# Threshold attention, then a mixture of attention experts: second-stage scores over all 128 rows, from copies made by DMA

## The chip, the core and the metric

The kernel runs on one core of a Trainium2 chip. What counts is device time in microseconds (us) from start to end of one execution. The kernel before took a median of 1035.93 us in three runs (1033.07 to 1035.97).

## What is computed

Stage 1 is attention over batch 8, 8 heads, 576 positions (S), head width 64 (D), where only scores within `tau` of the row's maximum count. Stage 2 reads stage 1's output as `x` (8, 576, 512) and runs four attention experts (E), causal, over it. A gate picks two experts for each position.

```python
scores = scale * q @ k.T;  keep where scores >= max - tau;  x = softmax(kept) @ v
logits = x @ w_gate;  w = softmax over the two largest
for e in range(4):
    q, k, v = x @ wq[e], x @ wk[e], x @ wv[e]
    a = softmax(causal(scale * q @ k.T))
    out += w[e] * (a @ v @ wo[e])
```

## The kernel before

Scores need more precision than one pass of the fast matmul type (fp32r) gives. So each operand is split in a high part (the value rounded to fp32r) and a low part (the rest), and a product is the sum of three: high x high, high x low, low x high (`HHL`, line 321). The contraction runs over the head width, 64, which is half of TensorE's 128 rows.

Stage 1 works on 32 pairs of heads (four for each batch `b`), each in five steps `s`: four query tiles of 128 rows (t = 0 to 3) and one tail tile of the 64 last positions of both heads (t = 4). Its main tiles already use all 128 rows: `prep` (line 245) copies by DMA the high part of the queries over itself (`qt`: both halves of the rows hold the two parts) and the keys twice (`kt`), so that two matmuls, [q_high; q_low] x [k_high; k_high] and [q_high; q_low] x [k_low; k_low], give the sum (line 342). These DMAs are issued by SyncE (SP), as are all loads and stores; SP works its DMAs off in order.

Stage 2 of batch `b` begins once the batch's last pair is done (`begin`, line 668) and its work is spread over the stage-1 steps of batch `b + 1`. `project` (line 445) makes queries and keys of one pair of experts (`ep` is 0 or 1): both experts of the pair lie one over the other, expert j in rows 64 j to 64 j + 63, and the high and low part side by side in the tiles `Q2[b, ep, i]` (i = 0 queries, 1 keys), four buffers in all. ScalarE (ACT) makes the high part, VectorE (DVE) the low part (line 474). `values` (line 481) makes the values and the gate. `scores2` (line 540) makes the scores of one query tile t for both experts: for t < 4 each expert has a PSUM bank, and three matmuls of (t + 1) x 128 columns over its 64 rows; the two experts are issued in turn, and then one mask matmul (bf16, 128 columns) in each bank. The tail tile takes six matmuls of 288 columns over all rows (line 564) and is not changed. Then follow exp, scaling by the gate (`scale2`, GpSimd), transposes (`transp2`), the product with the values (`attnv2`) and the output projection (`output`).

The order is written by a planner. `matmul` and `queued` (lines 152 to 159) add up a clock `pe[1]` of what each TensorE instruction is reckoned to cost (columns / 2.4 + 11 ns, half of that for 64 rows, 190 ns for a change of shape). Each stage-1 step gets a share of `STEP` = 5700 ns; `fill` (line 730) puts stage-2 pieces in until the step's goal is reached. `tiled` (line 734), called once in each of the steps s = 1 to 4, places one score tile; a tail tile is placed at the end of a step. Lists hold what is due: `S2` score tiles (order `T_MID` = 4, 3, 2, 1, 0, for the last batch `T_END`), `T2` transposes (due 7000 ns after the scores), `A2` and `O2`. After the last stage-1 step the loop at line 805 works off the last batch. The framework then orders the instructions of each engine's queue by priority and by what it reckons to be ready, so matmuls of one tile can be moved apart.

Loads: `load_pair` (line 178) loads a pair's keys and queries (`km`, `qm`, one buffer) and values (`vm` and `vtz`, three buffers, `VB` = 3).

Of the kernel before, what the change touches and what calls it, by code (L numbers as in the profile page):

```python
# [9 lines left out]
F32 = mybir.dt.float32  # L10
F32R = mybir.dt.float32r
# [15 lines left out]
MORE = (2, 3)  # L27

AFTER_S2, AFTER_V, AFTER_T2, AFTER_AV2 = 7000, 8500, 1800, 2000
BETWEEN_S2, AFTER_V_END = 2000, 5000  # L30

AV_AT = {4: (0, 3), 6: (3, 5)}
XBUFS = (2, 2, 1, 1)
# [3 lines left out]
E_W2 = "P"  # L37
W_AT = (5, 6, 7, 8)
CUT = 2
T_END = (2, 3, 4, 1, 0)  # L40
T_MID = (4, 3, 2, 1, 0)
E_XH = "A"
E_PT2 = "A"
# [3 lines left out]
PFB = 2  # L47
PR = {
    "max": -0.509, "thr": -0.091, "exp": 0.327, "stt": -2.461, "sum": -1.419, "nrm": 0.098,
# [6 lines left out]
PPB = 4  # L56
P2B = 3
PTB = 9
PTTB = 4
VB = 3  # L60
E_PTT = "A"


# [1 line left out]
def kernel(  # L65
# [13 lines left out]
    nc = tc.nc  # L79
# [3 lines left out]
    P = 128  # L83
# [94 lines left out]
    def load_pair(n):  # L178
        b, hp = divmod(n, NPAIR)
        hs = slice(2 * hp, 2 * hp + 2)  # L180
        vm = one.tile([P, 2, R, D], F32, tag="vm", name=f"vm_{n}", bufs=VB)
        pr("ld")
        def load(dst, src):
            r = nc.sync.dma_start(dst, src)
            if n in (1, 2):
                tc.add_manual_dep(r.ins, SPREAD[0].name, NOSYNC, reason="order")
        for t, x in ((km, k), (qm, q)):
            load(t[:, :, :R], x[b, hs, :SM, :].rearrange("h (p r) d -> p h r d", r=R))
            load(t[:ST, :, R], x[b, hs, SM:, :].rearrange("h s d -> s h d"))
        load(vm, v[b, hs, :SM, :].rearrange("h (p r) d -> p h r d", r=R))  # L190
        for j, rows in enumerate((slice(0, ST), slice(ST, P))):
            load(vtz[n % VB][rows, j], v[b, 2 * hp + j, SM:, :])
        VS[n] = (vm, vtz[n % VB])

# [245 lines left out]


    q2ds = [zeros(f"q2d{i}") for i in range(2)]
    Q2, V2, GW, GT = {}, {}, {}, {}

    def project(b, ep, cs):

        first, last = cs[0] == 0, cs[-1] == NC - 1
        for i, (wh, wl) in enumerate(((wqh, wql), (wkh, wkl))):
            if last:
                Q2[b, ep, i] = one.tile([P, 2, S], F32R, tag=f"q2{ep}{i}", name=f"q2_{b}_{ep}_{i}")  # L450
            t = Q2.get((b, ep, i))
            es = slice(ep * P, (ep + 1) * P)
            for hf in range(2):
                cols = slice(hf * HS, (hf + 1) * HS)
                g = gbank(f"pj_{b}_{ep}_{i}_{hf}_{cs[0]}")
                pr("pj")
                mm = [(w, c, x) for c in cs for w, x in ((wh, 0), (wh, 1), (wl, 0))]
                for n, (w, c, x) in enumerate(mm):
                    matmul(g[:, :HS], w[:, c, es], XT[b, c][x][:, cols],
                                     start=(n == 0), stop=(n == len(mm) - 1))  # L460
                pr("q2")
                if not last:
                    if b not in Q2:
                        Q2[b] = two.tile([P, EP, 4, HS], F32, tag="kt", name=f"part_{b}")
                    copy(E_Q2, Q2[b][:, ep, 2 * i + hf], g[:, :HS])
                    yield 3 * len(cs) * HS
                    continue
                src = g[:, :HS]
                if not first:
                    src = Q2[b][:, ep, 2 * i + hf]  # L470
                    nc.vector.tensor_tensor(src, g[:, :HS], src, op=ALU.add)
                hi, lo = t[:, 0, cols], t[:, 1, cols]
                copy(E_Q2, hi, src)
                nc.vector.tensor_tensor(lo, src, hi.bitcast(F32), op=ALU.subtract)
                if i == 0 and hf == 1:
                    for j in range(2):
                        sl = slice(j * D, (j + 1) * D)
                        copy(E_QD, q2ds[ep][sl, :, j * ST:(j + 1) * ST], t[sl, :, SM:].bitcast(F32))
                yield 3 * len(cs) * HS
# [58 lines left out]
    Z = {}  # L538

    def scores2(b, t, ep):  # L540
        q2, k2 = Q2[b, ep, 0], Q2[b, ep, 1]
        nmx = small.tile([P, 2], F32, tag="nmx", name=f"nm2_{b}_{ep}_{t}")
        sm = small.tile([P, 2], F32, tag="sm", name=f"sm_{b}_{ep}_{t}")
        pr("s2")
        if t < R:
            w = (t + 1) * P
            if b == B - 1:
                g = ps_s.tile([P, 2, 512], F32, tag="s", name=f"s2_{b}_{t}_{ep}")
                gg = [g[:, j] for j in range(2)]
            else:  # L550
                gg = [gbank(f"s2_{b}_{t}_{ep}_{j}") for j in range(2)]
            for i, (x, y) in enumerate(HHL):
                for j in range(2):
                    sl = slice(j * D, (j + 1) * D)
                    matmul(gg[j][:, :w], q2[sl, x, t * P:w], k2[sl, y, :w], start=(i == 0), stop=False)
            for j in range(2):
                matmul(gg[j][:, t * P:w], ident_b, mask, start=False, stop=True)
            views = [g[:, :w] for g in gg]
        else:
            w = S  # L560
            g = ps_s.tile([P, 2, 512], F32, tag="s", name=f"s2_{b}_{t}_{ep}")
            for hf in range(2):
                cols = slice(hf * HS, (hf + 1) * HS)
                for i, (x, y) in enumerate(HHL):
                    matmul(g[:, hf, :HS], q2ds[ep][:, x], k2[:, y, cols],
                                     start=(i == 0), stop=(hf == 0 and i == 2))
            matmul(g[:, 1, HS - ST:HS], ident_b, mask2, start=False, stop=True)
            views = [g[:, :, :HS]]
        p2 = two.tile([P, 2 * SM], F32, tag="p2" if b < B - 1 else "pp", name=f"p2_{b}_{t}_{ep}",
                      bufs=P2B if b < B - 1 else PPB)  # L570
        for j, sv in enumerate(views):
            pr("nm2")
            nc.vector.tensor_reduce(nmx[:, j:j + 1], sv, axis=AX.X if t < R else AX.XY, op=ALU.max, negate=True)  # L573
            pr("p2")
            nc.scalar.activation(p2[:, j * SM:j * SM + w] if t < R else halves(p2[:, :S]), sv, AF.Exp, bias=nmx[:, j:j + 1],  # L575
                                 accum_out=sm[:, j:j + 1])
        P2[b, t, ep] = (p2, sm, w, len(views))
# [97 lines left out]
    def project_some():  # L675

        while proj:
            b, what, g = proj[0]
            if what == "v" and left.get(b - 1, 0) or any(x[1] == b - 1 and what == f"q{x[3]}" for x in S2):
                return False  # L680
            try:
                next(g)
                return True
            except StopIteration:
                proj.pop(0)
                if what[0] == "q":
                    S2.extend((0, b, t, int(what[1])) for t in (T_MID if b < B - 1 else T_END))
                elif what == "v":
                    T2[len(T2) - len(unscaled):] = [(pe[1] + (AFTER_V if now[0] < N else AFTER_V_END), *x) for x in unscaled]
                    while unscaled:  # L690
                        scale2(*unscaled.pop(0))
        return False

    def score_tile():
        _, b, t, ep = S2.pop(0)
        scores2(b, t, ep)
        if b in GW and not unscaled:
            scale2(b, t, ep)
        else:
            unscaled.append((b, t, ep))  # L700
        T2.append((pe[1] + AFTER_S2, b, t, ep))
# [32 lines left out]
    def tiled():  # L734

        for _ in range(2):
            if due(A2):
                value_tile()
        if S2 and S2[0][2] < R and len(T2) < P2B:
            score_tile()  # L740

    now[0] = -10
# [8 lines left out]
    for _ in prep(0):  # L751
        pass
    load_pair(1)
    pre = iter(())
    goal = 0.0
    for i in range(N + 2):
# [24 lines left out]
        if slot:  # L781
            m, at = (n, 4) if s == 4 else (n - 1, 6)
            if 0 <= m < NPR:
                attnv(m, TS[slice(*AV_AT[at])])
                if at == 6 and m % NPAIR == NPAIR - 1:
                    begin(m // NPAIR)
            tiled()
        else:
            next(tr, None)
            if s in MORE:  # L790
                tiled()
# [7 lines left out]
            proj.extend((B - 1, "p", project(B - 1, ep, range(CUT))) for ep in range(EP))  # L799
            proj.append((B - 1, "v", values(B - 1, range(CUT))))  # L800
        fill(goal)
        if S2 and S2[0][2] == R and len(T2) < P2B:
            score_tile()
        goal = min(goal, pe[1])

# [1 line left out]
    while proj or S2 or T2 or A2 or O2:  # L807
# [6 lines left out]
            value_tile()  # L814
        elif transposable():
            transpose_tile()
        elif S2 and len(T2) < (P2B if S2[0][1] < B - 1 else PPB) and pe[1] >= since:
            score_tile()
            since = pe[1] + BETWEEN_S2
        elif not project_some():  # L820
# [31 lines left out]
```

## Time and profile before

| | |
|---|---|
| median of 3 runs | 1035.93 us |
| the profiled execution | 1033.38 us |
| its span, first to last instruction | 1031.7 us |
| TensorE (PE) busy | 966.5 us, 94% |
| PE weight loads (PEld) | 863.5 us, 84% |
| VectorE (DVE) | 816.5 us, 79% |
| ScalarE (ACT) | 651.6 us, 63% |
| GpSimd (POOL) | 408.4 us, 40% |
| granted TensorE clock, mean | 0.99 |

Busy time of PE counts each matmul from its start to its modelled end; matmuls overlap, so the pitch from start to start says what one costs, not its duration. In the names of the trace `s<-q,q` are stage-2 score matmuls (t < 4), `s<-q,q2d` those of the tail tile, `s<-mask,ident_b` the mask, `s<-kt,qt` and `s<-hl,qd` the stage-1 scores, `t` and `tm` transposes, `pj` the projections, `av` products with values, `o` the output projection. A form such as 64*128 64x384 is the weights (rows * columns) and the moving operand.

### The profile page before, as it was taken

The page shows a single profiled execution, that of the slowest core. Times are in us where ns is not written, and L with a number is a line of the kernel's source. Part 1 is how long each engine was busy: PE and PEld are TensorE (multiplying, and loading weights), DVE is VectorE, ACT ScalarE, POOL GpSimd, SP SyncE. Part 2 cuts the span into 40 slices and gives each one's busy share as a digit, 9 for nine tenths or more (in the row PEclk, how much of TensorE's full clock was granted, in tenths as well). Part 3 has the DMA queues.
Part 4 walks back from the last instruction along what each step waited for, and adds up shares of the span by engine and source line. Part 5 has one row for each costly group of instructions (what it writes and reads, how often), then busy time and mean ns, then how long its engine had stood idle before and what let it go on. Part 6 is the DMA issues. An engine that isn't in the chain of part 4 may idle for free.

```text
span 1031.7 us, 26572 instructions
## 1 busy us (share of the span) xinstructions
PE 966.5 (94%) x9520; PEld 863.5 (84%) x9520; DVE 816.5 (79%) x2374; ACT 651.6 (63%) x1564; POOL 408.4 (40%) x700
## 2 busy tenths in 40 slices
PE   4778999999999999999999999999999999999998
PEld 3676898789888898888987898978988889888975
DVE  4778688877888779888789878887788877988564
ACT  3667566765667656765667656676566765676554
POOL 2556424533244334443344332453324533433122
PEclk9998999999999999999999999999999999999999
DMA  6555423344223443225343242334322344311101
GB/s 156 142 128 141 121 73 91 102 117 119 59 72 95 133 112 93 61 68 143 90 103 94 72 124 75 91 102 126 110 56 73 96 132 112 79 30 44 42 2 46
DMA packets 83891, 96.11 MB, mean 93 GB/s; under 512 B 29745, under 2 KB 54321, under 8 KB 83761
## 3 DMA queue, kind: packets, MB, share of 16 engines
q1 hardware_dynamic: 83296, 93.83, 34.5%
q8 instruction: 76, 1.25, 0.5%
q10 hardware_dynamic: 464, 0.59, 0.2%
q14 instruction: 55, 0.44, 0.1%
HBM read 30.42 MB, written 9.44 MB: 39 GB/s over the span
## 4 chain that ended last, share of the span: by engine, by line
PE 59%; DVE 17%; ACT 13%; issue 5%; POOL 4%; DMA 1%; SPq 0%; DVEq 0%; ACTq 0%; POOLq 0%
PE av L159 18%; PE s L159 13%; PE tm L162 8%; PE pj L159 7%; DVE pp L356 5%; PE v L159 4%; PE o L159 4%; ACT p L575 3%; ACT pp L354 3%; PE t L162 3%; DVE nmx L349 3%; DVE x L439 2%; ACT pt L144 2%; PE qkT L162 2%; POOL pp L364 2%
## 5 line engine op out<-in xcount | busy, mean ns | idle before, releaser
L364 POOL TENSOR_SCALAR pp<-pp,ss 128x576 f32<-128x576 f32 x288 | 212.8, 750 | 408.4 <-DVE ss L370 313.0
L356 DVE SCALAR_TENSOR_TENSOR pp<-s,thr,pp 128x576 f32<-128x576 f32 x288 | 233.0, 814 | 77.3 <-ACT pp L354 72.5
L354 ACT ACTIVATE pp<-s,nmx 128x576 f32<-128x576 f32 x288 | 213.7, 746 | 80.6 <-DVE nmx L349 76.8
L349 DVE TENSOR_REDUCE nmx<-s 128x1 f32<-128x576 f32 x288 | 215.8, 751 | 41.6 <-PE s L159 40.4
L159 PE MATMUL s<-kt,qt 128*128 128x288 f32 x1024 | 205.3, 319 | 5.8 <-DMA qt<-hl 5.4
L162 PE MATMUL tm<-ident,pp 128*128 128x128 f32 x1152 | 166.2, 278 | 22.1 <-POOL pp L364 15.8
L159 PE MATMUL av<-pt,vm 128*64 128x128 f32 (+1 forms) x2560 | 167.8, 267 | 0.0
L159 PEld LDWEIGHTS s<-kt,qt 128*128 128x128 f32 x1024 | 151.9, 194 | 15.5 <-DMA qt<-hl 5.7
L162 PEld LDWEIGHTS tm<-ident,pp 128*128 128x128 f32 x1152 | 136.1, 143 | 33.2 <-POOL pp L364 22.6
L159 PEld LDWEIGHTS av<-pt,vm 128*64 128x64 f32 x2560 | 140.0, 138 | 15.4 <-issue 11.4
L144 ACT COPY pt<-tm 128x512 f32<-128x512 f32 x199 | 113.6, 589 | 58.6 <-PE tm L162 56.3
L575 ACT ACTIVATE p<-s,nm 128x384 f32<-128x384 f32 (+3 forms) x144 | 78.9, 551 | 63.4 <-DVE nm L573 59.0
L589 POOL TENSOR_SCALAR p<-p,sm,gw 128x512 f32<-128x512 f32 (+3 forms) x128 | 77.1, 610 | 81.4 <-ACT pt L144 35.4
L140 ACT ACTIVATE x<-av 128x256 fp32r<-128x256 f32 (+1 forms) x96 | 48.0, 500 | 71.5 <-PE av L159 49.6
L573 DVE TENSOR_REDUCE nm<-s 128x1 f32<-128x384 f32 (+3 forms) x144 | 71.1, 513 | 24.2 <-PE s L159 21.4
L162 PE MATMUL t<-ident,p 128*128 128x128 f32 x384 | 61.1, 284 | 15.9 <-DVE ss L369 8.9
L159 PE MATMUL av<-ptt,vtz 128*64 128x128 f32 (+1 forms) x640 | 68.8, 263 | 0.0
L140 ACT ACTIVATE pt<-t 128x512 f32<-128x512 f32 (+2 forms) x112 | 57.9, 541 | 15.6 <-PE t L162 14.2
L159 PE MATMUL v<-wvh,x 128*128 128x260 f32 x320 | 64.8, 287 | 0.0
L162 PEld LDWEIGHTS t<-ident,p 128*128 128x128 f32 x384 | 43.0, 144 | 25.9 <-POOL p L589 14.3
L439 DVE TENSOR_TENSOR x<-av,x 128x256 fp32r<-128x256 f32 (+1 forms) x96 | 47.6, 495 | 19.2 <-ACT x L140 16.0
L159 PE MATMUL av<-pt,v 128*64 128x128 f32 (+1 forms) x896 | 57.9, 262 | 1.9 <-ACT p L575 1.2
(132 smaller groups left out, 1808.9 us busy)
## 6 DMA issues: line engine op xcount, KB each, us to landing
kt<-hl SPq DMA_DIRECT2D x252, 144.0 KB, 2.7
qt<-hl SPq DMA_DIRECT2D x128, 128.0 KB, 2.4
km<-in_k_dram SPq DMA_DIRECT2D x32, 256.0 KB, 3.0
qm<-in_q_dram SPq DMA_DIRECT2D x32, 256.0 KB, 3.2
vm<-in_v_dram SPq DMA_DIRECT2D x32, 256.0 KB, 2.8
out_dram<-ob SPq DMA_DIRECT2D x32, 256.0 KB, 2.4
km<-in_k_dram SPq DMA_DIRECT2D x32, 32.0 KB, 2.7
qm<-in_q_dram SPq DMA_DIRECT2D x32, 32.0 KB, 2.7
```

The source lines that it names most:

```text
L140: nc.scalar.activation(dst, src, AF.Copy)
L144: nc.any.tensor_copy(dst, src)
L159: queued(nc.tensor.matmul(out, x, y, **kw), x, ns if x.shape[0] == P else ns / 2)
L162: queued(nc.tensor.transpose(out, x, ident), x, 109)
L349: nc.vector.tensor_reduce(nmx[:, js], sv, axis=AX.XY, op=ALU.max, negate=True)
L354: nc.scalar.activation(e, sv, AF.Exp, bias=nmx[:, js])
L356: nc.vector.scalar_tensor_tensor(e, sv, thr[:, js], e, op0=ALU.is_ge, op1=ALU.mult, accum_out=ss[:, js])
L364: nc.gpsimd.tensor_scalar(p, p, ss[:, h:h + 1], 0.0, op0=ALU.mult, op1=ALU.add)
L439: nc.vector.tensor_tensor(xl, gs, xh.bitcast(F32), op=ALU.subtract)
L573: nc.vector.tensor_reduce(nmx[:, j:j + 1], sv, axis=AX.X if t < R else AX.XY, op=ALU.max, negate=True)
L575: nc.scalar.activation(p2[:, j * SM:j * SM + w] if t < R else halves(p2[:, :S]), sv, AF.Exp, bias=nmx[:, j:j + 1], accum_out=sm[:, j:j + 1])
L589: nc.gpsimd.tensor_scalar(p, p, sm[:, j:j + 1], gg[:, j:j + 1], op0=ALU.mult, op1=ALU.mult)
```

## The change

- `scores2` for t < 4 takes two matmuls over 128 rows for each expert in place of three over 64. The experts come one after the other, each with its mask behind its two matmuls.
- `spread2` makes the operands: twelve DMAs on SP for each pair of experts, 64 rows of 512 columns each (128 KB): the queries' high over low part (`q2x`), the keys' high over high and low over low (`k2x`). There is one buffer of each (`X2`). For the last pair of the last batch the free stage-1 buffers `qt` and `kt` are taken.
- `spread_next` issues these DMAs when the head of `S2` comes to another pair of experts. A score tile with t < 4 may be placed only `AFTER_SPREAD` = 6000 ns of the planner's clock later (`scorable`); tail tiles may at once.
- `Q2` has two buffers in place of four, so the queries and keys of pair 1 are projected into those of pair 0; `project_some` holds a projection until all score tiles left in `S2` are no tails and have their copies.
- `VB` is 2. Values are loaded by `load_values` in step s = 1, behind the `attnv` that last reads the buffer.
- `T_END` is (4, 2, 3, 1, 0) in place of (2, 3, 4, 1, 0).

```diff
-BETWEEN_S2, AFTER_V_END = 2000, 5000
+BETWEEN_S2, AFTER_V_END, AFTER_SPREAD = 2000, 5000, 6000
-T_END = (2, 3, 4, 1, 0)
+T_END = (4, 2, 3, 1, 0)
-VB = 3
+VB = 2
...
+    X2 = (const.tile([P, 2, SM], F32R, name="q2x"), const.tile([P, 2, 2, SM], F32R, name="k2x"))
+    def spread2(b, ep):
+        qs, ks = Q2[b, ep, 0], Q2[b, ep, 1]
+        heads = [slice(j * D, (j + 1) * D) for j in range(2)]
+        q2x, k2x = X2 if (b, ep) != (B - 1, EP - 1) else (
+            two.tile([P, 2, SM], F32R, tag="qt", name="q2x_end"),
+            two.tile([P, 2, 2, S], F32R, tag="kt", name="k2x_end")[:, :, :, :SM])
+        Q2[b, ep] = (q2x, k2x)
+        pr("dm2")
+        for j, sl in enumerate(heads):
+            for x, rows in enumerate(heads):
+                for dst, src in ((q2x[rows, j], qs[sl, x, :SM]), (k2x[heads[0], j, x], ks[sl, x, :SM]),
+                                 (k2x[heads[1], j, x], ks[sl, x, :SM])):
+                    nc.sync.dma_start(dst.bitcast(F32), src.bitcast(F32))
...
-                Q2[b, ep, i] = one.tile([P, 2, S], F32R, tag=f"q2{ep}{i}", name=f"q2_{b}_{ep}_{i}")
+                Q2[b, ep, i] = one.tile([P, 2, S], F32R, tag=f"q2{i}", name=f"q2_{b}_{ep}_{i}")
...
-            for i, (x, y) in enumerate(HHL):
-                for j in range(2):
-                    sl = slice(j * D, (j + 1) * D)
-                    matmul(gg[j][:, :w], q2[sl, x, t * P:w], k2[sl, y, :w], start=(i == 0), stop=False)
             for j in range(2):
+                for i in range(2):
+                    matmul(gg[j][:, :w], q2x[:, j, t * P:w], k2x[:, j, i, :w], start=(i == 0), stop=False)
                 matmul(gg[j][:, t * P:w], ident_b, mask, start=False, stop=True)
...
-            if what == "v" and left.get(b - 1, 0) or any(x[1] == b - 1 and what == f"q{x[3]}" for x in S2):
+            if what == "v" and left.get(b - 1, 0) or what[0] == "q" and any(x[2] == R or (x[1], x[3]) != spread[0] for x in S2):
...
+    spread = [None, 0.0]
+    def spread_next():
+        if S2:
+            key = (S2[0][1], S2[0][3])
+            if key != spread[0]:
+                spread2(*key)
+                spread[:] = key, pe[1] + AFTER_SPREAD
+    def scorable(tail):
+        return S2 and (S2[0][2] == R) == tail and (tail or pe[1] >= spread[1])
...
-        if S2 and S2[0][2] < R and len(T2) < P2B:
+        if scorable(False) and len(T2) < P2B:
...
+            if s == 1 and n + 1 < NPR:
+                load_values(n + 1)
```

## Rows read from the trace of the kernel before

**Rows 1.** Windows: stretch, length, busy us (instructions) by engine, granted clock, DMA, GB/s.
```profile
508.00:630.00 122.00, 118.10 (x1188) 106.35 (x1189) 100.49 (x293) 79.51 (x192) 48.66 (x80) 1.00 0.37 96
966.00:1000.00 34.00, 31.72 (x294) 28.48 (x293) 20.43 (x65) 14.61 (x42) 6.26 (x10) 0.96 0.05 17
1000.00:1031.70 31.70, 26.81 (x240) 19.48 (x238) 14.50 (x45) 16.37 (x51) 8.73 (x17) 0.98 0.11 38
```
**Rows 2.** Waits of PE, 508 to 630 us: waited in total, times, longest.
```profile
PE t L162 <- DVE ss L369: 1.3, 1, 1.3
```
**Rows 3.** Timeline of PE, undisturbed score tiles: start, length (us), instructions merged.
```profile
581.18 0.33 PE L159 MATMUL s<-q,q 64*128 64x128 f32 x2
...
581.18 0.55 PE L159 MATMUL s<-q,q 64*128 64x128 f32 x6
581.66 0.28 PE L159 MATMUL s<-mask,ident_b 128*128 128x128 bf16 x2
581.76 0.79 PE L159 MATMUL s<-kt,qt 128*128 128x288 f32 x4
...
994.91 0.63 PE L159 MATMUL s<-q,q 64*128 64x256 f32 x6
...
639.83 0.80 PE L159 MATMUL s<-q,q 64*128 64x384 f32 x6
...
630.37 0.96 PE L159 MATMUL s<-q,q 64*128 64x512 f32 x6
```
**Rows 4.** Timeline of PE, score tiles whose second bank came late.
```profile
540.78 0.80 PE L159 MATMUL s<-q,q 64*128 64x256 f32 x6
...
560.94 1.21 PE L159 MATMUL s<-q,q 64*128 64x384 f32 x6
...
569.47 0.62 PE L159 MATMUL s<-q,q 64*128 64x256 f32 x3
570.34 0.61 PE L159 MATMUL s<-q,q 64*128 64x256 f32 x3 [0.26 <-DVE zl L642]
```
**Rows 5.** Timeline of PE, matmuls over all 128 rows.
```profile
992.31 0.96 PE L159 MATMUL s<-q,q2d 128*128 128x288 f32 x6
993.11 0.20 PE L159 MATMUL s<-mask,ident_b 128*128 128x64 bf16 x1
993.15 0.51 PE L159 MATMUL pj<-x,wkh 128*128 128x288 f32 x2
...
572.54 0.40 PE L159 MATMUL o<-wol,zh 128*128 128x512 f32 x1
572.78 0.39 PE L159 MATMUL o<-woh,zl 128*128 128x512 f32 x1
...
625.40 1.04 PE L162 MATMUL tm<-ident,pp 128*128 128x128 f32 x8
```
**Rows 6.** The page, part 6: DMA issues, KB each, median us to landing.
```profile
qt<-hl SPq DMA_DIRECT2D x128, 128.0 KB, 2.4
```
**Rows 7.** Timeline of SP and DVE around the projection of expert pair 0.
```profile
617.79 0.46 DVE L474 TENSOR_TENSOR q<-pj,q 128x288 fp32r<-128x288 f32 x1 [0.59 <-ACT q L140]
...
619.68 2.48 SPq L282 DMA_DIRECT2D qt<-hl  x4
622.20 1.28 SPq L184 DMA_DIRECT2D km<-in_k_dram  x2
```
**Rows 8.** Timeline of PE and SP around expert pair 0's last tile and pair 1's first.
```profile
549.27 1.13 SPq L184 DMA_DIRECT2D vtz<-in_v_dram  x2
...
548.92 0.55 PE L159 MATMUL s<-q,q 64*128 64x128 f32 x6
...
555.21 0.96 PE L159 MATMUL s<-q,q 64*128 64x512 f32 x6
...
555.63 6.59 SPq L282 DMA_DIRECT2D kt<-hl  x8
...
574.61 0.38 PE L159 MATMUL s<-kt,qt 128*128 128x288 f32 x1
```

More of the change, by code (lines that the diff above doesn't have):

```diff
@@ L180, in load_pair @@
         hs = slice(2 * hp, 2 * hp + 2)
-        vm = one.tile([P, 2, R, D], F32, tag="vm", name=f"vm_{n}", bufs=VB)
         pr("ld")
@@ L189, in load_pair, with load_values, load @@
             load(t[:ST, :, R], x[b, hs, SM:, :].rearrange("h s d -> s h d"))
-        load(vm, v[b, hs, :SM, :].rearrange("h (p r) d -> p h r d", r=R))
+    def load_values(n):
+        b, hp = divmod(n, NPAIR)
+        vm = one.tile([P, 2, R, D], F32, tag="vm", name=f"vm_{n}", bufs=VB)
+        pr("ld")
+        def load(dst, src):
+            r = nc.sync.dma_start(dst, src)
+            if n < 2:
+                tc.add_manual_dep(r.ins, SPREAD[0].name, NOSYNC, reason="order")
+        load(vm, v[b, 2 * hp:2 * hp + 2, :SM, :].rearrange("h (p r) d -> p h r d", r=R))
         for j, rows in enumerate((slice(0, ST), slice(ST, P))):
@@ L540, in scores2 @@
     def scores2(b, t, ep):
-        q2, k2 = Q2[b, ep, 0], Q2[b, ep, 1]
         nmx = small.tile([P, 2], F32, tag="nmx", name=f"nm2_{b}_{ep}_{t}")
@@ L545, in scores2 @@
         if t < R:
+            q2x, k2x = Q2[b, ep]
             w = (t + 1) * P
@@ L564, in scores2 @@
                 for i, (x, y) in enumerate(HHL):
-                    matmul(g[:, hf, :HS], q2ds[ep][:, x], k2[:, y, cols],
+                    matmul(g[:, hf, :HS], q2ds[ep][:, x], Q2[b, ep, 1][:, y, cols],
                                      start=(i == 0), stop=(hf == 0 and i == 2))
@@ L687, in project_some @@
                     S2.extend((0, b, t, int(what[1])) for t in (T_MID if b < B - 1 else T_END))
+                    spread_next()
                 elif what == "v":
@@ L696, in score_tile @@
         scores2(b, t, ep)
+        spread_next()
         if b in GW and not unscaled:
@@ L753 @@
     load_pair(1)
+    load_values(0)
     pre = iter(())
@@ L784 @@
                 attnv(m, TS[slice(*AV_AT[at])])
+            if s == 1 and n + 1 < NPR:
+                load_values(n + 1)
+            if 0 <= m < NPR:
                 if at == 6 and m % NPAIR == NPAIR - 1:
@@ L801 @@
         fill(goal)
-        if S2 and S2[0][2] == R and len(T2) < P2B:
+        if scorable(True) and len(T2) < P2B:
             score_tile()
@@ L816 @@
             transpose_tile()
-        elif S2 and len(T2) < (P2B if S2[0][1] < B - 1 else PPB) and pe[1] >= since:
+        elif S2 and scorable(S2[0][2] == R) and len(T2) < (P2B if S2[0][1] < B - 1 else PPB) and pe[1] >= since:
             score_tile()
```

2 rows, old and new, of the table PR are left out of this document.

## The prediction

> **What bounds the kernel now.** I read the windows by stage first, then the waits of PE inside one batch, then the timeline of PE at each of the 64 score tiles that change, and last SP's timeline around the places where the new copies come. In the middle of the run PE is busy for 118.10 of 122 us at the full clock, DVE for 100.49, ACT for 79.51 [rows 1]; PE's longest wait there is 1.3 us, once [rows 2]. So PE's issue sets the time of a batch: a matmul fewer is gained, a stop of PE is lost. The end is different: from 966 us on PE is busy for 31.72 of 34 us and then 26.81 of 31.7 [rows 1], which leaves 7.2 us idle; there chains count as well.
>
> What a score tile costs is read from pitches. In an undisturbed tile the two experts' half-row matmuls start together: two have started by 581.20, and six of 128 columns end 0.55 us after the first start, with the masks 0.48 us after it and the next matmul 0.58 us after it [rows 3]. The masks start 0.07 us before the last score matmul ends, and the next matmul 0.10 us after them, so a tile costs its row's length plus 0.03 us: 0.58, 0.66, 0.83 and 0.99 us for 128, 256, 384 and 512 columns [rows 3], together 3.06 us. This overlap is lost where the second expert's PSUM bank comes late: 1.21 us against 0.80 at 384 columns, 0.80 against 0.63 at 256, and 1.48 us (569.47 to 570.95) against 0.63 at 256 [rows 3, 4]. In each of the seven batches 0 to 6, each of the three happens about once (8, 7 and 7 times); in the last batch the timeline shows no such tile.
>
> **The change, part by part.**
>
> *Matmuls.* Full-row pitches: 0.11 us for 128 columns ((1.04 - 0.27) / 7 in eight transposes, 0.27 the length of the last, an estimate), 0.133 for 288 (six in 0.80), 0.235 for 512 [rows 5]. Between them I put 0.12 for 256 and 0.177 for 384. A mask inside full-row work costs 0.04 us to the next start, and that matmul then takes 0.08 longer: two matmuls of 288 last 0.51 us where 0.133 + 0.295 are due [rows 5]. A tile after is four matmuls, a mask between at 0.12 and one behind at 0.04: 0.60, 0.64, 0.87 and 1.10 us, together 3.21. So six matmuls become four and an undisturbed set of four tiles still gets 0.15 us dearer; 16 sets make +2.4 us. (Full rows save some 0.15 us a tile of change between half and full rows, and lose the overlap.)
>
> What is gained is the lost overlap: 0.41 + 0.17 + 0.85 = 1.43 us a batch. Part of the third is a real wait, as its second bank is free only 0.87 us after the first start, when the two matmuls and the mask of the first expert are over at 0.36; then the tile still costs 0.87 + 0.24 + 0.04 = 1.15 us, 0.51 above an undisturbed one, and only 0.34 of the 0.85 comes back. Bounds: 0.92 to 1.43 a batch, 6.5 to 10.0 over seven. I take 8.4 (1.2 a batch), as the tiles of pair 1 fall into other steps (below). Net of the 2.4: **-6.0 us** (-4.1 to -7.6).
>
> The Trainium skill ("TensorEngine Tiling (Array Packing)", Theoretical Speedup) says that a contraction of at most 64 rows can gain up to 2x from row tiling, which speaks against this change; its Key Properties say that a change of the tiling mode drains the engine, which speaks for it. The trace shows both: starts together, and 0.48 us for three overlapped starts where 0.33 would do. The first rule alone is rival C.
>
> *Copies for pair 0.* Twelve DMAs of 128 KB like `qt`'s: four take SP 2.48 us, 0.62 each [rows 7], and one lands 2.4 us after its issue [rows 6]. They come behind the low part of the keys, ready at 618.25, and behind SP's running copies for stage 1, which end at 622.16 [rows 7]. The first six, which are all that expert 0 needs, land at 622.2 + 5 x 0.62 + 2.4 = 627.7; the last at 631.4. Tile t = 3 stands at 630.37 [rows 3], over 6000 ns later also by the planner, so it stays in its step. Expert 1's matmuls come 2 x 0.235 + 0.04 us later, at 630.9: 0.5 us too early. Bounds: none, if the framework puts other matmuls ahead; 3.1 us, if the next pair's four loads (two take 1.28 us [rows 7]) go ahead of the copies. Over seven batches 0 to 22 us; by the nearest row 3.5, and I take **+2**, since in these queues matmuls move apart where an operand is late.
>
> *Copies for pair 1.* There is one `X2`, so SP must wait until t = 0 of pair 0 has run (548.92 to 549.47), and the values' load moved to this step stands ahead until 550.4 [rows 8]. The first six land at 555.9, the last at 559.6. By the charges of lines 152 to 162 for what stands between them, the next step's call of `tiled` comes 4 to 5 us of the planner's clock after t = 0, less than 6000 ns, so t = 3 does not stand at 555.21 [rows 8] any more but one step on, where t = 2 stands now, 560.94 [rows 4], and each later tile of pair 1 moves one step. Its work ends before the next batch's begins, so this costs nothing; its cover is other stage-2 pieces. Bounds: 0, to 3.9 us a batch (expert 1 wanted at 555.7, landed at 559.6) if it stays in its step, 27 us in all. Value taken: **0**, with 0.8 us to spare.
>
> What is queued behind on SP: `kt`'s and `qt`'s copies for the next pair. At 555.63 they start up to 1.6 us late and would end at about 567 instead of 564.8; first used at 574.61 [rows 8]. Loads of keys and queries slip by up to 7.4 us, and values are loaded a pair ahead; no one waits at once. Q2's two buffers hold the projection of pair 1 until pair 0's copies are read: in the middle this comes some 20 us later, nothing.
>
> The Trainium skill ("DMA: Bandwidth & Descriptors", Issuing engines are not separate DMA queues) calls the sequencer's time to initiate a DMA usually small relative to the DMA. Here twelve issues take 7.4 us and one landing 2.4, so the trace disagrees. By the page the copies would land some 3 us after they start and the +2 would be 0.
>
> *The end.* After pair 0's queries and keys of the last batch, the tail, the values and half of pair 1's projection cover the 6000 ns; then copies land up to 11 x 0.62 + 2.4 = 9.2 us after the start, 3 us late for expert 1. Pair 1's projection must also wait for these copies before it is written back. But the values and the gate end earlier than now (only one score tile ahead instead of two), and 7.2 us of idle time are there to take it up. Bounds: -3 (half of that idle) to +6 (9.2 less the 3.2 us that four projection pieces of six 0.133 us cover). I take **+0.5**.
>
> *Start and two value buffers:* values of a pair are read a pair later; nothing, bounds -0.3 to +0.3, half a DMA issue.
>
> **Sum.** 1033.38 - 6.0 + 2.0 + 0 + 0.5 = 1029.9 us. The profiled execution is 2.5 us below the median shown; two of three runs lie there. I add 1.1 for that: **1031 us**.
>
> **Rivals.**
>
> A, *no change*: the late banks stay late under the new order, so that 0.92 a batch comes back (net -4.1) and pair 0's copies cost the 3.5 of the nearest row: 1033.38 - 4.1 + 3.5 + 0.5 = 1033.3. For it: PE still meets banks that others release. Against: the tiles move.
>
> B, *the score tiles wait on PE for the copies*. PE works in order, and behind a waiting score matmul stands the stage-1 work that sets the batch's time. With the loads ahead of pair 0's copies, 3.1 us a batch: 1033.38 - 6.0 + 21.7 + 0.5 = 1049.6; with pair 1 in its old step 1055. It decides from 1.2 us a batch on ((6.0 - 0.5 + 3.1) / 7). For it: only 0.5 us is missing for pair 0 as it is. Against: PE waits almost nowhere now.
>
> C, *half rows are simply cheaper*: if a set of four were worth three full-row matmuls for each width, not 3.06 us, four would cost a third more: 0.64 us a set (0.11 + 0.12 + 0.177 + 0.235), 10.3 over 16; with 8.4 back, 1033.38 + 10.3 - 8.4 + 2.5 = 1037.8. Against: the 0.48 us of rows 3.
>
> **Chances.** Forecast 0.50, A 0.23, B 0.22, C 0.05. About 0.3% (3.1 us) is what a measurement of this kernel can tell from no change. The forecast's own range is 1023 (-7.6, no wait, -3 at the end) to 1032; A is "same", B and C slower. With A and the lower half of B the range is 1023 to 1048. Faster 0.50, same 0.23, slower 0.27.
>
> **What would show it.** Matmuls named `s<-k2x,q2x`: 256 of 128*128; a 512-column tile about 1.1 us and a 128-column tile about 0.6 us to the next matmul. SP: twelve issues in 7.4 us. PE's waits: little put down to the copies. t = 3 of pair 1 about 11 us behind t = 0 of pair 0. The distance between the same stage-1 step of two batches some 0.6 us shorter ((6.0 - 2.0) / 7) shows the loop's part. The prediction is wrong if PE waits over 1.2 us a batch for the copies, or if the last 65 us get more than 6 us longer.

## The result, and the profile after

The changed kernel takes 1024.62 us (median of 4 runs, 1023.74 to 1025.70); the kernel before took 1035.68 beside it. The ratio is 0.9899, 95% interval 0.988 to 0.9918. Forecast were 1031 us, with a range of 1023 to 1048: the direction and the range held, but the gain is more than twice the forecast one (1.0% against 0.45%).

The profiled execution takes 1023.74 us, its span 1021.6. Where the 10 us between the spans lie is seen by cutting both at the start of the fifth and of the last pair of heads (the first matmul `s<-hl,qd` of each pair): the first four pairs take 110.6 us before and 107.2 after, the loop 828.0 and 812.5, the end 93.0 and 102.0.

Windows of the kernel after: the start, one batch, the end. Columns as in [rows 1].
```profile
0.00:107.00 107.00, 76.65 (x708) 66.77 (x708) 75.20 (x214) 64.36 (x128) 53.92 (x117) 0.95 0.58 149
...
497.70:620.10 122.40, 118.25 (x1177) 107.71 (x1176) 103.84 (x299) 77.69 (x187) 48.46 (x80) 0.99 0.48 121
919.70:1021.60 101.90, 91.24 (x801) 77.53 (x800) 60.75 (x184) 52.12 (x149) 26.19 (x43) 0.98 0.24 63
```
The same view of the kernel before, start and end (a batch stands in [rows 1]).
```profile
0.00:111.00 111.00, 81.00 (x711) 71.06 (x712) 75.28 (x214) 64.56 (x129) 54.22 (x118) 0.92 0.58 146
...
939.00:1031.70 92.70, 85.48 (x769) 72.55 (x767) 56.21 (x168) 48.70 (x134) 22.11 (x37) 0.98 0.08 27
```
The start is no part of the change: there are no score tiles of the second stage in it, and PE's time for as many instructions follows the granted clock (0.92 and 0.95 of 2.4 GHz). A second profile of the changed kernel took 111.6 us for it, with a span of 1023.9, so only the medians and the time from the fifth pair on are compared below. The end is 9 us longer: PE has 32 more instructions and 5.8 us more work in it, which the loop did before, and its idle time rose from 7.2 to 10.7 us. The batch shown is the longest; the seven between the pairs 1 and 29 take 102.2 us (the first), then 120.5, 119.2, 120.2, 122.4, 120.5 and 121.9. Before, all but the first take 122.4 to 122.9. Part of the length of the two longest, 122.4 and 121.9, is TensorE's clock. Right behind PE's waits for copies (1.00 and 1.42 us here, 2.0 us two batches later) the granted clock is at half, 1.2 GHz, for 3.4 us:
```profile
560.90:564.30 3.40, 3.38 (x16) 2.67 (x14) 2.40 (x7) 2.12 (x6) 0.75 (x1) 0.50 0.55 166
```
By an estimate (work that takes 3.4 us at half the clock takes 1.7 at the full one) the two stretches cost some 3 us. The second profile has none in the loop, and its two batches take 121.2 and 120.6 us.

The group of the new score matmuls after (busy time, mean ns; idle time just before them and what ended it):
```profile
L159 PE MATMUL s<-k2x,q2x 128*128 128x384 f32 (+3 forms) x240 | 64.9, 361 | 14.0 <-DMA q2x<-q 8.3 <-ACT p L598 2.4 <-ACT ptt L140 1.5
```
240 and not 256: the last pair of the last batch has tiles of its own name. Of PE's idle time of 14.0 us in front of them, 9.3 us are waits for the copies (8.3 on `q2x`, 1.0 on `k2x`).

An undisturbed 512-column tile after, in PE's timeline (start, length, instructions):
```profile
505.88 0.73 PE L159 MATMUL s<-k2x,q2x 128*128 128x512 f32 x2
506.45 0.23 PE L159 MATMUL s<-mask,ident_b 128*128 128x128 bf16 x1
506.49 0.71 PE L159 MATMUL s<-k2x,q2x 128*128 128x512 f32 x2
507.04 0.23 PE L159 MATMUL s<-mask,ident_b 128*128 128x128 bf16 x1
507.08 0.77 PE L159 MATMUL s<-kt,qt 128*128 128x288 f32 x4
```
It costs 1.20 us to the next matmul, where six half-row matmuls cost 0.99 [rows 3] and 1.10 were forecast. The others of this batch take 0.97, 0.75 and 0.64 us. By the starts of all matmuls from the fifth pair on (idle time counted apart), score tiles with all masks (those of the tail tiles too, 0.7 us) hold 59.6 us before and 63.3 us after. So the part of the change that was to give the gain gives none.

SP and PE around the second pair of experts in the batch shown, after:
```profile
545.74 4.38 SPq L290 DMA_DIRECT2D qt<-hl  x4
550.22 0.55 SPq L468 DMA_DIRECT2D q2x<-q  x1
550.81 1.23 SPq L468 DMA_DIRECT2D k2x<-q  x2
552.09 0.61 SPq L468 DMA_DIRECT2D q2x<-q  x1
552.74 2.61 SPq L468 DMA_DIRECT2D k2x<-q  x2
555.45 0.54 SPq L468 DMA_DIRECT2D q2x<-q  x1
556.03 1.34 SPq L468 DMA_DIRECT2D k2x<-q  x2
557.41 0.59 SPq L468 DMA_DIRECT2D q2x<-q  x1
558.05 1.24 SPq L468 DMA_DIRECT2D k2x<-q  x2
```
```profile
556.53 0.40 PE L159 MATMUL s<-k2x,q2x 128*128 128x512 f32 x1
557.93 0.47 PE L159 MATMUL s<-k2x,q2x 128*128 128x512 f32 x1 [1.00 <-DMA k2x<-q]
559.90 0.47 PE L159 MATMUL s<-k2x,q2x 128*128 128x512 f32 x1 [1.42 <-DMA q2x<-q]
```
The twelve issues take 9.1 us and the matmuls come into the middle of them. PE's waits over the whole run after:
```profile
PE s L159 <- DMA q2x<-q: 8.3, 6, 2.0
...
PE s L159 <- DVE pp L364: 4.9, 14, 0.6
```
With one wait of 1.0 us on `k2x`, PE waits 9.3 us for copies. All of it stands at tile t = 3 of the second pair of experts, in the batches 1 to 6. Yet the waits that came once a batch before are gone from batch 1 on, though smaller ones on DVE's `pp` have come, and that is what the experiments are about.

### The profile page after: what moved, and what is told of

It reads as the page before. It is cut to its first block, busy times and chain, and to the rows that moved or that the text cites. A ratio compares the mean times of both kernels' runs of the same rounds, so it can differ in the third digit from the quotient of the medians.

```text
span 1021.6 us, 26701 instructions
## 1 busy us (share of the span) xinstructions
PE 955.8 (94%) x9392; PEld 862.3 (84%) x9392; DVE 830.7 (81%) x2403; ACT 641.5 (63%) x1535; POOL 406.5 (40%) x699
## 4 chain that ended last, share of the span: by engine, by line
PE 72%; DVE 10%; ACT 8%; issue 3%; POOL 3%; DMA 2%; SPq 2%; DVEq 0%; POOLq 0%; ACTq 0%
PE av L159 20%; PE s L159 16%; PE tm L162 9%; PE pj L159 9%; PE o L159 5%; PE v L159 5%; PE t L162 4%; PE qkT L162 2%; ACT p L598 2%; DVE pp L364 2%; DVE nm L596 2%; ACT pp L362 2%; DVE nmx L357 2%; ACT x L140 1%; DVE x L447 1%
## 5 line engine op out<-in xcount | busy, mean ns | idle before, releaser
L159 PE MATMUL s<-kt,qt 128*128 128x288 f32 x1024 | 203.1, 317 | 10.5 <-DMA qt<-hl 5.4
L159 PEld LDWEIGHTS s<-kt,qt 128*128 128x128 f32 x1024 | 151.2, 193 | 21.6 <-DVE pp L364 9.6
L159 PE MATMUL av<-pt,vm 128*64 128x128 f32 (+1 forms) x2560 | 162.2, 266 | 0.0
L159 PEld LDWEIGHTS av<-pt,vm 128*64 128x64 f32 x2560 | 135.5, 137 | 13.7 <-issue 8.2
L144 ACT COPY pt<-tm 128x512 f32<-128x512 f32 x170 | 97.4, 588 | 51.8 <-PE tm L162 51.0
L598 ACT ACTIVATE p<-s,nm 128x576 f32<-128x576 f32 (+3 forms) x144 | 78.6, 549 | 60.2 <-DVE nm L596 57.0
L596 DVE TENSOR_REDUCE nm<-s 128x1 f32<-128x576 f32 (+3 forms) x144 | 71.7, 514 | 18.5 <-PE s L159 16.1
L159 PE MATMUL s<-k2x,q2x 128*128 128x384 f32 (+3 forms) x240 | 64.9, 361 | 14.0 <-DMA q2x<-q 8.3
L159 PE MATMUL av<-ptt,vtz 128*64 128x128 f32 (+1 forms) x640 | 64.5, 263 | 0.0
L359 DVE SCALAR_TENSOR_TENSOR thr<-nmx,tau_p 128x1 f32<-128x1 f32 x288 | 58.2, 205 | 2.1
```

The lines of the kernel that those rows point to most:

```text
L144: nc.any.tensor_copy(dst, src)
L159: queued(nc.tensor.matmul(out, x, y, **kw), x, ns if x.shape[0] == P else ns / 2)
L359: nc.vector.scalar_tensor_tensor(thr[:, js], nmx[:, js], -1.0, tau_p, op0=ALU.mult, op1=ALU.subtract)
```

## Experiments

The theories at the start: **rows** (PE gains from four full-row matmuls instead of six half-row ones), **order** (the gain comes from where the second stage's tiles are put: one pair of experts at a time, due 6000 ns after the copies), **copies** (what they cost, and how). Each kernel was timed beside the kernel before on the same chip; medians of before there were 1032 to 1033 us.

**1. The value loads alone.** Before, with the two value buffers and the moved loads.
```diff
-VB = 3
+VB = 2
```


> The kernel before with two value buffers and the values' loads moved to step 1, nothing else. Theory 'values' (SP no longer stands in the way): 1029 to 1033. Theories 'shape' and 'order': no change, 1033 to 1036. The first four pairs, in which no score tile changes, took 107.2 us after and 110.6 before: if the loads do that, it shows here; if TensorE's clock did it, the granted clock of the first 40 us tells.


Measured 1032.34 us, ratio 1.0005 (0.999 to 1.002). This part costs and gives nothing, as predicted.

**2. The order alone.** After, with the copies left out and `scores2` again as in the kernel before, half rows straight from the projection; four buffers for it.
```diff
-                    matmul(gg[j][:, :w], q2x[:, j, t * P:w], k2x[:, j, i, :w], start=(i == 0), stop=False)
+                    matmul(gg[j][:, :w], q2x[sl, x, t * P:w], k2x[sl, y, :w], start=(i == 0), stop=False)
```


> The changed kernel's planner (gates, 6000 ns, tail tile first at the end, two value buffers), but score tiles with half-row matmuls straight from the projections (four buffers of these again) and no copies. Theory 'order' (pair 1's tiles a step later is what pays): 1020 to 1026, as fast as the changed kernel or faster, as half rows cost some 3 us less and no copy is waited for. Theory 'shape' (full rows pay): 1033 to 1037.


Measured 1021.22 us, ratio 0.9887 (0.9862 to 0.9912): at least as fast as the change itself, without full rows and without a copy.

**3. The rows without the new order.** After, with no delay and the old `T_END`.
```diff
-AFTER_SPREAD = 2000, 5000, 6000
+AFTER_SPREAD = 2000, 5000, 0
```


> The changed kernel with a delay of 0 in place of 6000 ns and the old order of the last batch: full rows and copies, pair 1's tiles in their old steps. Theory 'order': the gain goes and PE waits for the copies at the first tile of pair 1, 3.9 us a batch: 1035 to 1055. Theory 'shape': some 1025 plus the waits for copies, unless the framework moves other matmuls ahead.


Measured 1054.52 us, ratio 1.021 (1.018 to 1.0241). PE's waits in it:
```profile
PE t L162 <- DVE ss L377: 8.9, 7, 1.3
PE tm L162 <- ACT pt L144: 7.5, 7, 1.2
PE s L159 <- DVE pp L364: 7.5, 14, 0.6
...
PE s L159 <- ACT p L598: 5.0, 8, 2.4
PE tm L162 <- DVE pt L144: 3.8, 7, 0.6
PE s L159 <- DMA q2x<-q: 2.3, 5, 0.6
...
PE s L159 <- DMA k2x<-q: 1.9, 1, 1.9
...
PE s L159 <- DMA k2x_end<-q: 0.9, 1, 0.9
```
Waits put down to the copies (the last three rows) sum to only 5.1 us. The first row is as in the kernel before. The price appears in the four rows between, on ACT and DVE: they sum to 23.8 us, and PE has at most 0.3 us of each in the kernel of experiment 6, which has no delay and no copies either. This fits stage-2 softmax that stands late in the queues of DVE and ACT and holds up stage-1 work behind it. But full rows and the old `T_END` differ there too, so that the copies are the cause is likely and not shown.

**4. The copies left out.** After, without the copies; the score tiles read zeros in the place of queries and keys, so the second stage's scores are not computed.


> The changed kernel without the 192 copies: score tiles read zeros (left out: the copies, so stage-2 scores mean nothing). It prices copies and the waits for them. If the copies cost what PE's waits on them say (about 9.3 us in six or seven waits): 1013 to 1018. If the framework would fill those waits anyhow: 1021 to 1025.


Measured 1006.41 us, ratio 0.9744 (0.9718 to 0.9771). From the fifth pair on PE is idle for 15.9 us instead of 31.7. So the copies cost some 18 us.

**5. The same with half rows in turn** (again zeros instead of queries and keys).


> As the kernel without copies (score tiles read zeros, left out: the copies and with them the stage-2 scores), but with half-row matmuls, three per expert in turn. It prices the shape alone, with the same order and nothing to wait for. If the pitches say it all (half rows 0.5 us cheaper for a set of four): 1000 to 1006, against 1006.4. Theory 'shape' (full rows pay): 1012 to 1022.


Measured 1021.98 us, ratio 0.9894 (0.9871 to 0.9917). Experiment 2 with real operands took 1021.22, so zeros in their place do not change the time. This seemed to give the rows 15.6 us. But the score tiles take 61.3 us here and 60.5 in experiment 4. And PE's order of work is that of experiment 2, not of 4: the planner charges the two forms of a tile differently (lines 152 to 162) and places the rest by it. Experiments 11 and 12 take this apart.

**6. The order without its delay.** Experiment 2 with `AFTER_SPREAD` at 0.


> As the order-only kernel (half rows, no copies), but with a delay of 0 in place of 6000 ns, so that pair 1's tiles stand in their old steps; the held projections, the new order of the last batch and the values stay. Theory 'the delay pays': 1030 to 1034. Theory 'the held projections or the last batch pay': 1019 to 1023.


Measured 1031.16 us, ratio 0.9989 (0.9975 to 1.0003). In the batches 0 to 6 the score tiles start where they start in the kernel before, within 0.4 us. Of the order, the delay of 6000 ns is what pays.

**7. Eight larger copies instead of twelve.**
```diff
-                for dst, src in ((q2x[rows, j], qs[sl, x, :SM]), (k2x[heads[0], j, x], ks[sl, x, :SM]),
-                                 (k2x[heads[1], j, x], ks[sl, x, :SM])):
+                for dst, src in ((q2x[rows, j], qs[sl, x, :SM]), (k2x[rows, j], ks[sl, :, :SM])):
```


> The changed kernel with eight DMAs for a pair of experts instead of twelve: a key copy takes the high and low part at once. If SP's issues (0.62 us each) are what PE waits for, the last copy lands 2.5 us earlier and most of the 9 us of waits on copies go: 1016 to 1021. If the waits only move: 1023 to 1026.


Measured 1062.28 us, ratio 1.0269 (1.0227 to 1.0311): a miss. Its DMA issues (KB each, median us to landing), then PE's longest wait:
```profile
k2x<-q SPq DMA_DIRECT2D x60, 256.0 KB, 4.3
q2x<-q SPq DMA_DIRECT2D x60, 128.0 KB, 3.6
```
```profile
PE s L159 <- issue: 21.9, 7, 3.3
```
After, each of the twelve lands in 2.4 us, and the last of them mostly 9 to 12 us after the first issue; merged, the last one lands no earlier (mostly 10 to 13 us). In one batch DVE and PE do this (the bracket is idle time and what ended it):
```profile
705.75 0.69 DVE L595 TENSOR_REDUCE nm<-s 128x1 f32<-128x512 f32 x1 [1.39 <-PE s L159]
706.36 1.41 DVE L357 TENSOR_REDUCE nmx<-s 128x1 f32<-128x576 f32 x2
...
708.97 1.78 PE L159 MATMUL s<-kt,qt 128*128 128x288 f32 x6 [3.26 <-issue]
```
DVE waits for the matmuls of a score tile to take its maximum, and the maxima of the stage-1 scores come behind it. PE goes on 3.26 us later. The profile puts this stop to no engine; that it ends when the stage-1 softmax frees PE's `s` banks fits the order of these rows and is not shown. The clock pays too. Around the stop the granted clock falls to half:
```profile
708.10:714.90 6.80, 5.93 (x25) 5.40 (x26) 4.99 (x16) 2.75 (x6) 1.02 (x2) 0.50 0.23 70
```
Between 148 and 964 us there are eight such stretches, 41 us in all (two of 3.4 us in the changed kernel's loop), worth up to 20 us of the 38 by the estimate above.

**8. One expert after the other.** Experiment 2, and then the kernel before, with the three half-row matmuls of one expert ahead of those of the other, so that they can't overlap. A theory of mine was that full rows had gained because the two experts no longer take turns.
```diff
-            for i, (x, y) in enumerate(HHL):
-                for j in range(2):
-                    sl = slice(j * D, (j + 1) * D)
+            for j in range(2):
+                sl = slice(j * D, (j + 1) * D)
+                for i, (x, y) in enumerate(HHL):
```


> The order-only kernel (delay, half rows, no copies), but with one expert after the other: three half-row matmuls and the mask, then the other expert's. The overlap of half rows is given up, some 0.3 to 0.5 us a tile. Theory 'turn' (finishing one expert before the other begins is what made full rows 15.6 us faster without copies): 1006 to 1014. Theory 'rows' (it is the full rows): 1024 to 1040, as 64 tiles lose their overlap.

> The kernel before, with nothing changed but the order of the matmuls in a score tile: one expert after the other, half rows. Theory 'turn': faster than before even in the old order of tiles, 1022 to 1030. Theory 'rows', or if it takes the new order of tiles too: 1033 to 1045.


Measured 1037.58 us, ratio 1.0044 (1.0025 to 1.0063), and 1041.95 us, ratio 1.0094 (1.0072 to 1.0115). The score tiles hold 100.8 and 99.9 us instead of 60.6 and 59.6: the overlap of half rows is worth 40 us of PE's time in the tiles. Of this 9 us appear in the time of the kernel before, and PE's idle time falls from 31.3 to 15.5 us. But this edit moves the tiles as well. The planner sees two more changes of shape in a tile, 380 ns by its charges. In batch 2 the tiles stand 5 to 19 us later than before, the loop is 13 us shorter and the end 22 us longer. So the 9 us are not the overlap's price alone.

**9. Full rows with the experts in turn**, zeros as in experiment 4.


> The kernel without copies (score tiles read zeros; left out: the copies), full rows, but with the experts in turn and the masks last, as half rows had them. Theory 'turn': back to 1018 to 1023. Theory 'rows': stays at 1004 to 1009.


Measured 1005.72 us, ratio 0.974 (0.9723 to 0.9758), as in 4. The theory of turns falls.

**10. A later second stage.** After, with 9000 ns, then with 12000.


> The changed kernel with a delay of 9000 ns in place of 6000. If the copies cost the time that PE waits for them and what the framework moves ahead meanwhile, they have landed by then: 1012 to 1020. If a step later starves other stage-2 work, above all at the end: 1026 to 1035.

> The after kernel with the second stage's work due 12000 ns after the copies were issued instead of 6000 ns (9000 ns gave 1012.5 us). Theory 'the later start pays because the copies have landed': at 9000 ns PE's waits on copies are nearly gone, so 12000 ns gives nothing more, 1009 to 1016 us. Theory 'spreading pays by itself': another 3 to 10 us, 1002 to 1009 us. Rival: the second stage now runs past its batch and meets the next one's due times; slower than at 9000 ns, 1016 to 1030 us.


Measured 1012.47 us, ratio 0.9804 (0.9788 to 0.982), and 1017.19 us, ratio 0.9854 (0.9836 to 0.9872). A batch at 9000 ns:
```profile
495.80:613.70 117.90, 115.44 (x1179) 105.85 (x1175) 99.19 (x294) 79.91 (x193) 48.63 (x80) 1.00 0.49 127
```
4.6 us less than before, and in the whole run PE waits for a copy once, for 0.2 us. In this batch the 512-column tile of the second pair of experts stands 7.4 us into a pair of heads; after, it stands at 1.4. At 12000 ns the batches are shorter still at first (116.4 us) and longer at the end (120.2).

**11. Half rows with the charges of full rows.** Experiment 2, with only the planner's clock changed.
```diff
+            start = pe[1] + (190 if pe[2] != (P, P) else 0)
...
+            pe[1], pe[2] = start + 4 * (w / 2.4 + 11) + 120, (P, P)
```


> The kernel of e2 (half rows, the new order, no copies), with one difference: the planner's bookkeeping of TensorE after a score tile is set to what it charges for a full-row tile, four runs of (w/2.4 + 11) ns and 120 ns, with no price for a change of tile shape. The instructions of a tile are the same as in e2. Theory 'charges' (the 15.6 us between e4 and e5 come from where the planner puts the other work): the time falls from e2's 1021 us to that of e4, 1003 to 1010 us. Theory 'rows' (they come from TensorE): it stays at 1021 us, 1017 to 1025. About 1014 would give half to each.


Measured 1011.57 us, ratio 0.9794 (0.977 to 0.9818). With the same instructions for a tile, another placement takes off 9.7 us against experiment 2.

**12. Full rows with the charges of half rows**, zeros as in 4.


> The kernel of e4 (full rows, the copies left out, the score tiles read zeros in the place of the copied queries and keys, so the second stage's scores are not computed), with one difference: the planner's bookkeeping after a score tile is set to what it charges for half rows, three runs of (w/2.4 + 11) ns, 120 ns and two changes of shape of 190 ns. Theory 'charges': the time rises from e4's 1006 us to e5's 1022 us, 1018 to 1025. Theory 'rows': it stays at 1006 us, 1003 to 1010.


Measured 1014.33 us, ratio 0.9823 (0.9806 to 0.9839): in the middle. So of the 15.6 us between 5 and 4 the charges make 8 to 10, the rows 5 to 8. As the score tiles take 60.9 us here and 61.3 in 5, the rows' part does not lie in the tiles. By the starts of all matmuls it is spread over small amounts at many places (4 us on `s<-kt,qt`, 3 on `t<-ident,p`, 2 on `tt<-ident,pp`), and I found no single cause.

**13. The charges alone, and other delays.** The two lines of 11 in the kernel before; then the kernel of 11 with 4000 and with 9000 ns.


> The kernel before (no later start, no copies, half rows), with one difference: the planner's bookkeeping after a score tile is set to what it charges for a full-row tile. Theory 'the charges pay by themselves': about 10 us below before, 1020 to 1026 us. Theory 'they pay only on top of the later start': the time of before, 1030 to 1035 us. Theory 'any other order falls somewhere else by chance': either, or slower than before.

> The kernel of e12 with the second stage's work due 4000 ns after the projection instead of 6000 ns (e12: 1011.6 us; at 9000 ns, e14: 1023.2 us). Theory 'there is one best delay, which the copies push to a later one': a smooth curve, 1010 to 1017 us. Theory 'the later the better up to the point of the jam': 1014 to 1024 us, on the way to e6. Theory 'chance': anything from 1000 to 1030 us.

> The kernel of e12 with the second stage's work due 9000 ns after the projection's copies instead of 6000 ns. Theory 'charges', if the later start pays without the copies as it did with them (e10: 1012.5 against 1024.6 us, 12 us): below e12, 995 to 1006 us. If the later start only paid because it let the copies land: no gain on e12, within 3 us of it. Theory 'rows': 1010 to 1021 us, by the later start alone.


Measured 1033.61 us, ratio 1.0002 (0.9986 to 1.0019); 1029.78 us, 0.9973 (0.9956 to 0.9989); 1023.17 us, 0.9911 (0.9886 to 0.9936). The charges pay only on top of the delay. Without copies the best of the three delays is 6000 ns; with copies the best of 0, 6000, 9000 and 12000 is 9000.

What the delay and the charges take away is seen in PE's waits between 230 and 900 us (in total, times, longest), first of the kernel before:
```profile
PE t L162 <- DVE ss L369: 6.4, 5, 1.3
PE pj L159 <- ACT ptt L140: 3.4, 6, 0.6
PE tm L162 <- ACT p L575: 2.0, 5, 0.4
PE t L162 <- DVE x L439: 2.0, 5, 0.6
PE tm L162 <- POOL p L589: 1.6, 5, 0.3
```
and of the kernel of experiment 11:
```profile
PE t L162 <- DVE hl L277: 5.7, 9, 0.9
PE t L162 <- ACT p L589: 1.8, 4, 0.5
```
Before, five small waits come about once in each of the five batches here, in the two pairs of heads that hold six of a batch's eight score tiles. With the second stage later they shrink or go, though one on DVE's `hl` takes their place in part.

What the two numbers do is to move all eight tiles, and each run settles into one of a few placings. The table gives, by the starts of the matmuls, where tile t = 3 of the first pair of experts stands in the fourth batch, counted from the start of its first pair of heads, and how long the batches are from the fourth on.

| t = 3 at | kernels | batch |
|---|---|---|
| 30.2 us | before; no delay (6); charges alone (13); charges, 4000 ns (13) | 122.3 to 122.7 us |
| 39.2 us | charges, 6000 ns (11) | 119.1 to 119.3 |
| 39.2 us | full rows, no copies (4) | 118.4 |
| 39.2 us | the change | 120.5 to 122.5 |
| 48.7 us | half rows, 6000 ns (2) | 121.4 to 122.4 |
| 48.5 us | charges, 9000 ns (13) | 120.7 to 121.0 |
| 48.4 us | the change with 9000 ns (10) | 117.8 |

So 4000 ns moves nothing. Experiment 2 wins in the first three batches (119.5, 117.5 and 118.3 us). In the fourth its tiles have slipped to another placing, and a batch is nearly as long as before; in two such batches 3.4 us at half the granted clock add to it (from 567.6 and 690.5 us). With the charges of full rows (11) the tiles do not slip.

A second run of the changed kernel gave 1025.04 us, ratio 0.9927 (0.9906 to 0.9948).

## Why the prediction was wrong

The runs give the chain below (median us; time from the fifth pair's start, and PE's idle time in it, by the profile).

| kernel | median | from pair 5 on | PE idle in it |
|---|---|---|---|
| before | 1033 | 921.0 | 31.3 |
| the new order with no delay (6) | 1031.2 | 920.2 | 31.3 |
| + delay of 6000 ns (2) | 1021.2 | 910.2 | 21.6 |
| + charges of full rows (11) | 1011.6 | 902.1 | 17.7 |
| + full rows, copies left out (4) | 1006.4 | 894.4 | 15.9 |
| + copies: the change | 1024.6 | 914.5 | 31.7 |

So the change is about -27 us and +18 us, in a sum that had -6.0 and +2.5 for them.

- **Matmuls, forecast -6.0: wrong.** This is the first step that failed. Score tiles and masks hold 3.7 us more, not 6.0 less. An undisturbed set of four costs 3.57 us (0.64, 0.75, 0.97, 1.21) where I had 3.21. The term that was too small is the first matmul of a tile. I gave it its plain pitch, 0.235 us at 512 columns, and in the timeline above it takes 0.34 (0.57 to the mask, less 0.235). The second expert's first takes 0.31 there, as forecast with the 0.08 behind a mask. Sixteen sets make +8.1 us instead of +2.4. Of the disturbance before (59.6 less 16 x 3.06, 10.6 us) 4.4 come back, half of the 8.4 forecast. What full rows do give, 5 to 8 us, appears outside the tiles.
- **"Each later tile of pair 1 moves one step ... so this costs nothing", value 0: wrong in the move and in its worth.** It is the largest term: the delay takes off 10 us (from 6 to 2), and with the charges 20 (from 6 to 11). I had pair 0's t = 3 stay in its step and pair 1's tiles move by one step, some 6 us. Batch 0 is near that for pair 0 (within 1 us), and pair 1 moves by 3 to 11 us. But from batch 2 on all eight tiles stand later than before in their batch, pair 0's by 4 to 9 us and pair 1's by 8 to 20. And I had read the row `PE t <- DVE ss` of [rows 2] as a wait that PE hardly has, as the view was of one batch: over the run that and six more rows come seven times each, 3.4 us a batch. They went in each kernel whose tiles moved (2 and 11), and stayed where none moved (6). "PE's issue sets the time of a batch" led me to value a move at nothing unless a matmul goes.
- **Copies for pair 0, forecast +2, and for pair 1, forecast 0: together they cost 18 us.** At pair 0's tiles PE waits for no copy, so that term was 0. All 9.3 us of waits for copies are pair 1's. There the start was right (550.4 forecast and 550.22 measured), but the twelve issues take 9.1 us instead of 7.4, and the copies land later: the first six at 557.8 (555.9 forecast), the last at 561.1 (559.6 forecast). Moreover the copies start 4 us behind tile t = 0 (546.3 us), since SP still issues `qt`'s four, and not 1.5 us behind it as I worked out from [rows 8]. And t = 3 comes 10.2 us behind that tile; my rows gave 12.0 (560.94), my signs about 11, and only with the 11 is the spare time 0.8 us (with 12.0 it is 1.9). Instead PE waits 2.4. Only half of the 18 is waits on copies. PE's idle time grows by 15.8 us against experiment 4, so 6.5 us more are waits on other engines (DVE's `pp` 4.9 us against 2.4, POOL's `zl` 3.1 against none, DVE's `pt` 1.7 against none), and in this profile the two stretches at half the clock add some 3 us (an estimate, above). How a copy makes DVE or POOL late was not followed instruction by instruction. The Trainium skill ("DMA: Bandwidth & Descriptors", Issuing engines are not separate DMA queues) calls the time to initiate a DMA usually small relative to the DMA. Here one issue takes 0.76 us (9.1 / 12) beside a landing of 2.4, and twelve in a row set when the last lands.
- **The end, forecast +0.5: about 9 measured,** beyond the +6 of the bound, of which 5.8 us of PE's work is no loss but moved from the loop; the added idle time is 3.4 us. Without copies (experiment 4) the end takes 96.0 us instead of 102.0.
- **Start and value buffers: right** (experiment 1).
- **Rivals.** A (no change) is out by the interval. B (score tiles wait for the copies): PE's waits for copies are 1.3 us a batch, over the 1.2 at which B was to decide, and it still didn't turn the sign, as the later start was not in my sum. In its old step the price came out (1055 forecast, 1054.5 in experiment 3), by luck, as its mechanism did not: it had 27 us of waits for copies, and PE has 5.1 there, and more on ACT and DVE. C (half rows simply cheaper) is near the truth for the undisturbed tiles (+10.3 us, measured +8.1) and wrong for the kernel: without copies full rows are faster under either set of charges.

That 1031 came as near as it did, 6 us, is luck: two errors of opposite sign.

## What to carry to other kernels

A change that brings its own due times and planner charges is two changes; time the new order with the old instructions before the new instructions get the credit or the blame, and compare where the instructions stand in the trace, since a constant of the planner can move all of them or none. Where PE is 97% busy, waits that come once a batch are still worth adding up over the run, since a later start of the side work can remove them all at once. And after a copy is added, try the delay behind it again: 9000 ns instead of 6000 made the change worth 20 us instead of 7 to 11, by one number, and half rows with the charges of full rows, without any copy, gain as much (1011.57 us).

## What was not expected of the hardware

- Merging two 128 KB copies of 64 rows into one of 256 KB saved an issue but landed in 4.3 us instead of 2.4, and the 128 KB copies beside it in 3.6.
- Half-row matmuls of two experts save 40 of 100 us in their tiles when they alternate (experiment 8).
- The mean granted clock of the first 110 us differs between executions (0.88 to 0.95 of 2.4 GHz in the profiles here) where PE's work is the same and is broken by idle time. The part up to the fifth pair takes 113.2 us at 0.88 and 107.2 at 0.95, so a profiled span moves by up to 6 us.
- A wait can cost more than its length. In the changed kernel waits of 1.00 and 1.42 us (at 557.9 and 559.9 us), and in experiment 2 waits of 0.23, 0.38 and 0.54 us (from 565.1 to 567.2 us), were followed by 3.4 us at 1.2 GHz. Single waits for copies of 1.1 to 1.4 us in other batches of the changed kernel were not.
- A delay moves the time in jumps: 4000 to 6000 ns took off 18 us (13 and 11), 6000 to 9000 ns added 12. The jumps are those of the tiles' placing (table in 13): none moves at 4000. Why half rows are slower in the placing of 9000 ns, and full rows with copies are faster there, the runs don't show.
